# Queries and keys of a head pair: loaded as they lie, with the heads put side by side by GpSimd copies

## The chip, the cores and the metric

One core of a Trainium2 chip. The metric is the device time of one execution of the whole program in microseconds (us), as the median of several runs. The engines are named PE (TensorE), ACT (ScalarE), DVE (VectorE), POOL (GpSimd) and SP (the queue that issues most DMAs).

## What is computed

```python
def _attn_ref(q, k, v):                     # q, k, v: (4, 12, 448, 64) float32
    S = q.shape[2]
    scale = 1.0 / np.sqrt(q.shape[-1])
    scores = scale * np.matmul(q, k.transpose(0, 1, 3, 2)) - np.log(S)
    attn = 1.0 / (1.0 + np.exp(-scores))
    return np.matmul(attn, v).astype(np.float32)

def reference(**kwargs):
    ...
    x = np.ascontiguousarray(attn_out.transpose(0, 2, 1, 3)).reshape(B * S, H * D)   # 1792 x 768
    x = _moe_ref(x=x, **moe_kwargs)          # elu(x @ w_in) @ w_out, weights 768 x 2048 and 2048 x 768
    return _moe2_ref(x=x, **moe2_kwargs)     # (h - tanh(h)) @ w_out with h = x @ w_in
```

The four weight matrices arrive with eight bytes per element and are converted to float32 in the kernel.

## The kernel before

**Stages.** The kernel runs attention first, then the two MLPs, each as a Strassen-like product of blocks in which every float32 operand is split into a head and a rest (three matmuls for one product). While attention runs, the first MLP's weights are already loaded, converted, summed into blocks and stored to scratch memory in HBM. Attention lasts to about 197 us of the span.

**A pair of heads.** The 4 x 12 heads make 24 pairs. For each pair n the work is: transposes of q and k to bring the head dimension to the partitions (`transpose`, L302 to L309; key `t`, with w = 1 for k and 0 for q), a split into head and rest (`head` and `rest`, L311 to L324, on ACT and DVE), scores (`scores`, L332, key `s`), sigmoid (`sig`, L352, ACT at L358), products with v (`pv`, L362 to L373, matmul at L369) and a copy out (`xdone`, L374). One pair's time in the plan is `CYCLE` = 6900 ns. The transposes of pair n are planned two cycles before its scores.

**Loads of q and k.** Pairs are loaded in groups of NL = 2 (m = n // 2). Two buffers of q and k alternate between groups: the tile `first` and the tile `kq1` (L197 to L200). Both hold the two heads of a pair side by side for each row, so that a transpose takes 128 adjacent columns. A row of one head is 64 floats, 256 B, in HBM and in the buffer's place between the two heads. `ld_q` (L230) issues four DMAs for a group and `ld_k` (L213) three; each moves four heads, one row of every head into each partition. `ld_kr` (L222) brings the last 64 keys of each head and `ld_v`, `ld_vr` the values. Groups m > 0 use `ld_q` and `ld_k`; the first group has loads of its own (`ld_first`, L239). All these loads but a few of the first group are issued by SP.

**Order.** `Sched` is a planner: each operation has a queue, a cost, the operations it waits for and a due time (`PHASES`, L85). It simulates the queues and emits each engine's instructions in the planned order. Engines and queues then run their instructions strictly in that order, each waiting for its own semaphores. Attention's operations of one queue are also chained in order of due time (L413), SP's loads among them. A load of a group waits for the transposes of the group that used its buffer before (L287, L288).

**Weights beside attention.** `p_load` (DMA at L592) brings a block of the first MLP's second weights, 768 KB, into XB or XA; `p_narrow` converts it in three steps, the first on ACT (L541), the others on DVE (L544, L548); `p_sum` (L601) forms sums and `p_store` (L606) writes them to `p_forms`. Blocks of the first weights go through tile R1a (load at L530), L541 and so on, to `kept_wi` (L560). `first` is used again after attention: a kept block of weights is loaded into it (L528) and GpSimd writes sums into it (L661).

Of the kernel before, what the change touches and what calls it, by code (L numbers as in the profile page):

```python
# [16 lines left out]
class Sched:  # L17
# [73 lines left out]
    ("ldk",): 4000 - 5 * CYCLE, ("ldv",): 3300 - 2 * CYCLE,  # L91
# [8 lines left out]
def kernel(  # L100
# [67 lines left out]
    with tc.manual_schedule():  # L168
# [7 lines left out]
        def attention():  # L176
# [20 lines left out]
            n = 2 * NL * R * D  # L197
            kq = [first, ld_p.tile([128, 2 * n], F32, name="kq1")]
            kl = [t[:, :n].rearrange("p (c h d) -> p c h d", h=2 * NL, c=R) for t in kq]
            ql = [t[:SP, n:2 * n].rearrange("p (r h d) -> p r h d", h=2 * NL, r=R) for t in kq]  # L200
# [3 lines left out]
            for i in range(2):  # L204
                nc.gpsimd.memset(kl[i][RS:128, R - 1, 0::2, :], 0.0)
                nc.gpsimd.memset(kl[i][0:RS, R - 1, 1::2, :], 0.0)
# [6 lines left out]
            def ld_k(m, i0, i1):  # L213
                b, hp = pairs[NL * m]
                h0, h1 = 2 * hp + 2 * i0, 2 * hp + 2 * i1
                for c in range(3):
                    nc.sync.dma_start(
                        out=kl[m % 2][:, c, 2 * i0:2 * i1, :],
                        in_=k[b, h0:h1, 0:384].rearrange("h (p c) d -> c p h d", c=3)[c],
                    )  # L220

            def ld_kr(m):  # L222
                b, hp = pairs[NL * m]
                for j in range(2):
                    nc.sync.dma_start(
                        out=kl[m % 2][RS * j:RS * j + RS, R - 1, j::2, :],
                        in_=k[b, 2 * hp + j:2 * hp + 2 * NL:2, 384:S].rearrange("h p d -> p h d"),
                    )

            def ld_q(m, i0, i1):  # L230
                b, hp = pairs[NL * m]
                h0, h1 = 2 * hp + 2 * i0, 2 * hp + 2 * i1
                for r in range(R):
                    nc.sync.dma_start(
                        out=ql[m % 2][:, r, 2 * i0:2 * i1, :],
                        in_=q[b, h0:h1].rearrange("h (p r) d -> r p h d", r=R)[r],
                    )

            def ld_first(kind, i):  # L239

                b, hp = pairs[i]
                for j in range(2):
                    if kind == "k":
                        nc.sync.dma_start(
                            out=kl[0][:, :3, 2 * i + j], in_=k[b, 2 * hp + j, 0:384].rearrange("(p c) d -> p c d", c=3)
                        )
                    else:
                        (nc.sync if i else nc.scalar).dma_start(
                            out=ql[0][:, :, 2 * i + j], in_=q[b, 2 * hp + j].rearrange("(p r) d -> p r d", r=R)
# [23 lines left out]
            def loads(m):  # L273


                both = (0, NL)
# [1199 lines left out]
```

## Time and profile before

| | |
|---|---|
| time, median of 3 runs | 1025.57 us (1024.84 to 1026.34) |
| the profiled execution | 1025.25 us |
| its span, first to last instruction | 1023.5 us |
| PE busy | 990.7 us (97%), 5300 matmuls |
| DVE busy | 763.9 us |
| ACT busy | 600.8 us |
| POOL busy | 79.4 us, 74 instructions |
| mean granted TensorE clock | 0.992 |
| DMA packets | 171263, of these 58672 under 512 B |

Busy time counts instructions that an engine executes, not its issuing of DMAs and not its waits. The page says which engine works most over the whole program, and there PE is nearly full. It doesn't say what a single stage is held by: that is read from a stretch of the trace, from the waits of the engines in it and from the chain of work that ended last, which is followed back from the end to whatever released each step. Names such as `kq<-in_q_dram` mean: written tile, from what is read.

### The profile page before, as it was taken

The page shows a single profiled execution, that of the slowest core. Times are in us where ns is not written, and L with a number is a line of the kernel's source. Part 1 is how long each engine was busy: PE and PEld are TensorE (multiplying, and loading weights), DVE is VectorE, ACT ScalarE, POOL GpSimd, SP SyncE. Part 2 cuts the span into 40 slices and gives each one's busy share as a digit, 9 for nine tenths or more (in the row PEclk, how much of TensorE's full clock was granted, in tenths as well). Part 3 has the DMA queues.
Part 4 walks back from the last instruction along what each step waited for, and adds up shares of the span by engine and source line. Part 5 has one row for each costly group of instructions (what it writes and reads, how often), then busy time and mean ns, then how long its engine had stood idle before and what let it go on. Part 6 is the DMA issues. An engine that isn't in the chain of part 4 may idle for free.

```text
span 1023.5 us, 15546 instructions
## 1 busy us (share of the span) xinstructions
PE 990.7 (97%) x5300; PEld 855.4 (84%) x5300; DVE 763.9 (75%) x1155; ACT 600.8 (59%) x966; POOL 79.4 (8%) x74
## 2 busy tenths in 40 slices
PE   8969899989999999999999999999999999999998
PEld 6535455678888888888899998888888999999998
DVE  3657677898888888768878789777777779566673
ACT  4746567876666667666667565444444546445652
POOL 0000000012222220000000021111111000000000
PEclk9989899999999999999999999999999999999999
DMA  7889897025555569999994733555555894455442
GB/s 196 240 253 302 250 285 219 16 80 190 189 188 188 188 203 316 380 412 411 345 328 125 247 109 111 191 190 191 187 194 184 304 335 160 136 174 170 125 143 89
DMA packets 171263, 218.61 MB, mean 214 GB/s; under 512 B 58672, under 2 KB 129584, under 8 KB 170928
## 3 DMA queue, kind: packets, MB, share of 16 engines
q1 hardware_dynamic: 169616, 217.04, 63.8%
q8 instruction: 41, 0.67, 0.3%
q10 hardware_dynamic: 1568, 0.59, 0.2%
q14 instruction: 38, 0.31, 0.1%
HBM read 142.61 MB, written 74.97 MB: 213 GB/s over the span
## 4 chain that ended last, share of the span: by engine, by line
PE 89%; DMA 5%; DVE 3%; ACT 1%; issue 1%; SPq 1%; ACTq 0%; DVEq 0%
PE psa L746 12%; PE psd L746 11%; PE psx L746 9%; PE psu L901 7%; PE psv L901 7%; PE psw L901 7%; PE pvps L369 6%; PE psa L901 6%; PE psb L901 6%; PE psb L746 5%; PE psy L901 4%; PE sps L344 3%; PE psx L901 3%; DMA p_forms<-XB 2%; PE sps L309 2%; DMA R1a<-in_moe_w_in_dram 1%
## 5 line engine op out<-in xcount | busy, mean ns | idle before, releaser
L358 ACT ACTIVATE an<-sps,bias 128x896 f32<-128x896 f32 x72 | 67.3, 1005 | 34.1 <-PE sps L344 33.9
L873 ACT ACTIVATE XB<-t 128x384 fp32r<-128x384 f32 (+1 forms) x111 | 62.0, 563 | 40.8 <-PE psw L901 11.7
L877 DVE TENSOR_TENSOR XB<-t,XB 128x384 fp32r<-128x384 f32 (+1 forms) x111 | 68.3, 625 | 13.2 <-ACT XB L873 13.0
L661 POOL TENSOR_TENSOR second<-second 128x384 f32<-128x384 f32 x15 | 19.0, 1269 | 709.1 <-DVE second L548 213.6
L369 PE MATMUL pvps<-an,vl 128*64 128x448 f32 x288 | 62.7, 573 | 0.0
L873 ACT ACTIVATE XB<-spare 128x512 fp32r<-128x512 f32 (+1 forms) x72 | 41.1, 572 | 26.9 <-PE psw L901 6.6
L344 PEld LDWEIGHTS sps<-e 64*128 64x128 f32 x432 | 39.9, 189 | 18.9 <-PE pvps L369 15.5
L746 PE MATMUL psa<-XB,W 128*128 128x512 f32 x192 | 54.2, 391 | 0.0
L344 PE MATMUL sps<-e 64*128 64x448 f32 x432 | 51.3, 380 | 0.0
L877 DVE TENSOR_TENSOR XB<-spare,XB 128x512 fp32r<-128x512 f32 (+1 forms) x72 | 44.2, 621 | 9.2 <-ACT XB L873 8.8
L901 PE MATMUL psu<-XB,XB 128*128 128x384 f32 (+1 forms) x192 | 46.3, 348 | 0.0
L901 PE MATMUL psv<-XB,XB 128*128 128x384 f32 (+1 forms) x192 | 46.2, 348 | 0.0
L901 PE MATMUL psw<-XB,XB 128*128 128x384 f32 (+1 forms) x192 | 46.2, 348 | 0.0
L369 PEld LDWEIGHTS pvps<-an,vl 128*64 128x64 f32 x288 | 19.5, 144 | 28.5 <-issue 21.1
L746 PEld LDWEIGHTS psa<-XB,W 128*128 128x128 f32 x192 | 36.0, 188 | 7.5
L775 ACT ACTIVATE spare<-t 128x512 f32<-128x512 f32 (+1 forms) x33 | 19.0, 579 | 37.2 <-DVE t L763 36.1
L661 POOL TENSOR_TENSOR first<-first,second 128x384 f32<-128x384 f32 x30 | 40.1, 1335 | 1.2
L317 DVE CAST e<-sps 128x448 fp32r<-128x448 f32 x24 | 15.0, 624 | 30.4 <-PE sps L309 19.3
L746 PE MATMUL psd<-XB,W 128*128 128x512 f32 x144 | 35.7, 391 | 1.5 <-DVE W L678 1.3
L779 ACT ACTIVATE spare<-spare 128x512 f32<-128x512 f32 (+1 forms) x64 | 36.6, 572 | 0.7
L901 PE MATMUL psa<-XB,XB 128*128 128x384 f32 (+1 forms) x156 | 36.9, 347 | 0.0
L901 PE MATMUL psb<-XB,XB 128*128 128x384 f32 (+1 forms) x156 | 36.9, 347 | 0.0
(362 smaller groups left out, 2717.7 us busy)
## 6 DMA issues: line engine op xcount, KB each, us to landing
x_forms<-R1b SPq DMA_DIRECT2D x58, 256.0 KB, 2.0
first<-p_forms SPq DMA_DIRECT2D x36, 384.0 KB, 6.1
t<-x_forms SPq DMA_DIRECT2D x64, 192.0 KB, 2.9
t<-x_forms SPq DMA_DIRECT2D x47, 256.0 KB, 5.0
x_forms<-t SPq DMA_DIRECT2D x44, 256.0 KB, 2.0
x_forms<-R1b SPq DMA_DIRECT2D x58, 192.0 KB, 4.8
first<-in_moe_w_in_dram SPq DMA_DIRECT2D x14, 768.0 KB, 5.3
second<-in_moe_w_in_dram SPq DMA_DIRECT2D x14, 768.0 KB, 6.2
```

The costliest lines, as they stand in the source:

```text
L309: nc.tensor.transpose(ps[:, c * P:(c + 1) * P], t[:, c, h:h + 2, :], ident[:P, :P])
L317: nc.vector.tensor_copy(out=to, in_=x)
L344: nc.tensor.matmul(out=ps[:, j, :S], lhsT=e[lanes, ks, cols], rhs=e[lanes, qs, :S], start=(x == 0), stop=(x == 2),)
L358: nc.scalar.activation(out=a[:, :m], in_=T.pop(("s", n, u))[:, :m, :S], func=ACTF.Sigmoid, bias=bias, scale=scale)
L369: nc.tensor.matmul(out=ps[D * j:D * j + D], lhsT=vl[n // NL % NVL][:, n % NL, 5 * j + u if u < 3 else 3 + j], rhs=a[:, j if u < 3 else 0], ...
L661: by.tensor_tensor(out=out, in0=x, in1=y, op=op)
L746: nc.tensor.matmul(out=ps, lhsT=w[wz][:, k0:k0 + 128], rhs=xs[xz][:, kk], start=(opens and n == 0), stop=(n == 3 * KH - 1), skip_group_che ...
L775: nc.scalar.activation(out=r, in_=h, func=ACTF.Tanh)
L779: nc.scalar.activation(out=r, in_=r, func=ACTF.Exp, scale=-1.0)
L873: nc.scalar.activation(out=at_place(og_place[i, s, p, j], 0, i)[:, :HW[s]], in_=T["graw", i, s, p, j], func=ACTF.Copy)
L877: nc.vector.tensor_tensor(out=lo, in0=T.pop(("graw", i, s, p, j)), in1=f(hi), op=ALU.subtract)
L901: nc.tensor.matmul(out=T["o2", tag], lhsT=lhsT, rhs=rhs, start=(p in OPENS and j == 0 and x == 0), stop=(j == NG - 1 and x == 2), skip_gro ...
```

## The change

Groups m > 0 no longer use `ld_q` and `ld_k`. For each pair and each of q and k, one DMA (`ld_qk`) brings both heads in the rows in which they lie in HBM: four rows of q (1024 B) or three of k (768 B) of a head behind each other in one partition. They go to a new tile `raw_qk` with room for two pairs. A copy on GpSimd (`side_by_side`) then writes them into the layout that the transposes read, with the two heads side by side. The prepared q and k now have one buffer of two pairs, in the tile `first`; the last 64 keys (`krest`) keep two. The load of pair n waits for the copy of pair n - 2, the copy for its load and for the transposes of pair n - 2, and the transposes for the copy. In the plan the load is due at the pair's cycle less four, plus 1000 ns, the copies at less three, plus 4500 and 4600 ns. The first two pairs are loaded as before, straight into `first`.

```diff
--- before.py
+++ after.py
@@ -88,7 +88,7 @@
     ("sig", 0): 700, ("sig", 1): 1700, ("sig", 2): 2700, ("sig", 3): 3700,
     ("head", 1): 4400 - 2 * CYCLE, ("head", 0): 4900 - 2 * CYCLE,
     ("rest", 1): 5050 - 2 * CYCLE, ("rest", 0): 5700 - 2 * CYCLE, ("xdone",): CYCLE + 500,
-    ("ldk",): 4000 - 5 * CYCLE, ("ldv",): 3300 - 2 * CYCLE,
+    ("ldk",): 4000 - 5 * CYCLE, ("ldqk",): 1000 - 4 * CYCLE, ("side", 1): 4500 - 3 * CYCLE, ("side", 0): 4600 - 3 * CYCLE, ("ldv",): 3300 - 2 * CYCLE,
 }
 
 SHIFTS = {
@@ -194,46 +194,45 @@
                 out=ident, in_=ident, pattern=[[-1, 128]], compare_op=ALU.is_equal, fill=0.0,
                 base=0, channel_multiplier=1,
             )
-            n = 2 * NL * R * D
-            kq = [first, ld_p.tile([128, 2 * n], F32, name="kq1")]
-            kl = [t[:, :n].rearrange("p (c h d) -> p c h d", h=2 * NL, c=R) for t in kq]
-            ql = [t[:SP, n:2 * n].rearrange("p (r h d) -> p r h d", h=2 * NL, r=R) for t in kq]
+
+            DD = 2 * D
+            raw_qk = ld_p.tile([128, 4 * NL * R * D], F32, name="raw_qk")
+
+            def parted(t):
+                a, b = NL * R * DD, NL * (R + 3) * DD
+                return t[:SP, :a], t[:, a:b], t[:, b:b + NL * DD].rearrange("p (i x) -> p i x", i=NL)
+
+            (ql, kl, rest0), (qraw, kraw, rest1) = parted(first), parted(raw_qk)
+            krest = rest0, rest1
+            ql, kl = (t.rearrange("p (i c x) -> p i c x", i=NL, x=DD) for t in (ql, kl))
+            qraw, kraw = (t.rearrange("p (i h x) -> p i h x", i=NL, h=2) for t in (qraw, kraw))
             vl = [vs_p.tile([128, NL, 10, D], F32, name=f"vl{i}") for i in range(NVL)]
 
             es = [e0, ld_p.tile([128, 4, 512], F32R, name="e1")]
             for i in range(2):
-                nc.gpsimd.memset(kl[i][RS:128, R - 1, 0::2, :], 0.0)
-                nc.gpsimd.memset(kl[i][0:RS, R - 1, 1::2, :], 0.0)
+                nc.gpsimd.memset(krest[i][RS:128, :, :D], 0.0)
+                nc.gpsimd.memset(krest[i][0:RS, :, D:], 0.0)
             for i in range(NVL):
                 nc.gpsimd.memset(vl[i][RS:128, :, 3, :], 0.0)
                 nc.gpsimd.memset(vl[i][0:RS, :, 4, :], 0.0)
 
             T = {}
 
-            def ld_k(m, i0, i1):
-                b, hp = pairs[NL * m]
-                h0, h1 = 2 * hp + 2 * i0, 2 * hp + 2 * i1
-                for c in range(3):
-                    nc.sync.dma_start(
-                        out=kl[m % 2][:, c, 2 * i0:2 * i1, :],
-                        in_=k[b, h0:h1, 0:384].rearrange("h (p c) d -> c p h d", c=3)[c],
-                    )
+            def ld_qk(w, n):
+                b, hp = pairs[n]
+                x = k[b, 2 * hp:2 * hp + 2, 0:384].rearrange("h (p c) d -> p h (c d)", c=3) if w else q[b, 2 * hp:2 * hp + 2].rearrange("h (p r) d -> p h (r d)", r=R)
+                nc.sync.dma_start(out=(qraw, kraw)[w][:, n % NL], in_=x)
+
+            def side_by_side(n, w):
+                x = (qraw, kraw)[w][:, n % NL].rearrange("p h (c d) -> p c h d", d=D)
+                nc.gpsimd.tensor_copy(out=(ql, kl)[w][:, n % NL].rearrange("p c (h d) -> p c h d", h=2), in_=x)
 
             def ld_kr(m):
                 b, hp = pairs[NL * m]
                 for j in range(2):
                     nc.sync.dma_start(
-                        out=kl[m % 2][RS * j:RS * j + RS, R - 1, j::2, :],
+                        out=krest[m % 2][RS * j:RS * j + RS, :, D * j:D * j + D],
                         in_=k[b, 2 * hp + j:2 * hp + 2 * NL:2, 384:S].rearrange("h p d -> p h d"),
-                    )
-
-            def ld_q(m, i0, i1):
-                b, hp = pairs[NL * m]
-                h0, h1 = 2 * hp + 2 * i0, 2 * hp + 2 * i1
-                for r in range(R):
-                    nc.sync.dma_start(
-                        out=ql[m % 2][:, r, 2 * i0:2 * i1, :],
-                        in_=q[b, h0:h1].rearrange("h (p r) d -> r p h d", r=R)[r],
                     )
 
             def ld_first(kind, i):
@@ -242,11 +241,11 @@
                 for j in range(2):
                     if kind == "k":
                         nc.sync.dma_start(
-                            out=kl[0][:, :3, 2 * i + j], in_=k[b, 2 * hp + j, 0:384].rearrange("(p c) d -> p c d", c=3)
+                            out=kl[:, i, :, D * j:D * j + D], in_=k[b, 2 * hp + j, 0:384].rearrange("(p c) d -> p c d", c=3)
                         )
                     else:
                         (nc.sync if i else nc.scalar).dma_start(
-                            out=ql[0][:, :, 2 * i + j], in_=q[b, 2 * hp + j].rearrange("(p r) d -> p r d", r=R)
+                            out=ql[:, i, :, D * j:D * j + D], in_=q[b, 2 * hp + j].rearrange("(p r) d -> p r d", r=R)
                         )
 
             def ld_v(m, i):
@@ -273,10 +272,9 @@
             def loads(m):
 
 
-                both = (0, NL)
-                kinds = {"kfirst": lambda m, i: ld_first("k", i), "qfirst": lambda m, i: ld_first("q", i), "k": ld_k, "kr": ld_kr, "q": ld_q, "v": ld_v, "vr": ld_vr}
+                kinds = {"kfirst": lambda m, i: ld_first("k", i), "qfirst": lambda m, i: ld_first("q", i), "kr": ld_kr, "v": ld_v, "vr": ld_vr}
                 if m:
-                    jobs = [("q", both), ("k", both), ("kr", ()), ("v", (0,)), ("vr", ()), ("v", (1,))]
+                    jobs = [("kr", ()), ("v", (0,)), ("vr", ()), ("v", (1,))]
                 else:
                     ld_first("q", 0)
                     nc.scalar.activation(out=warm, in_=bias, func=ACTF.Sigmoid)
@@ -287,7 +285,7 @@
                     free = {"k": (2, ("t", 1)), "q": (2, ("t", 0)), "v": (NVL, ("pv", 3))}[kind[0]]
                     last = [(free[1][0], NL * (m - free[0]) + i) + free[1][1:] for i in range(NL)]
                     sch.op(
-                        ("ld" + kind, m) + args, "SP", 600 * {"kfirst": 2, "qfirst": 2, "k": 3, "kr": 2, "q": 4, "v": 1, "vr": 2}[kind],
+                        ("ld" + kind, m) + args, "SP", 600 * {"kfirst": 2, "qfirst": 2, "kr": 2, "v": 1, "vr": 2}[kind],
                         lambda kind=kind, args=args: kinds[kind](m, *args),
                         last, when("ldv" if kind[0] == "v" else "ldk", NL * m) + x, 2500,
                     )
@@ -296,7 +294,7 @@
                 m, i = divmod(n, NL)
                 if kind == "v":
                     return [("ldv", m, i), ("ldvr", m)]
-                part = ("ld" + kind, m, 0, NL) if m else ("ld" + kind + "first", 0, i)
+                part = ("side", n, "qk".index(kind)) if m else ("ld" + kind + "first", 0, i)
                 return [part] + ([("ldkr", m)] if kind == "k" else [])
 
             def transpose(n, w):
@@ -304,9 +302,9 @@
                     T["tps", n] = pss[(4 * n - 5) % 3].tile([128, 2, BK], F32, tag="s", name="sps")
                 T["t", n, w] = ps = T["tps", n][:, w]
                 P, t = ((SP, ql), (128, kl))[w]
-                t, h = t[n // NL % 2], 2 * (n % NL)
                 for c in range(R):
-                    nc.tensor.transpose(ps[:, c * P:(c + 1) * P], t[:, c, h:h + 2, :], ident[:P, :P])
+                    x = krest[n // NL % 2][:, n % NL] if w and c == 3 else t[:, n % NL, c]
+                    nc.tensor.transpose(ps[:, c * P:(c + 1) * P], x, ident[:P, :P])
 
             def head(n, w):
                 W, slot = ((S, 1), (512, 2))[w]
@@ -397,6 +395,9 @@
                     sch.op(("warm", 0), "PE", 100, lambda: keep_warm(WARM), [], -10 ** 9)
                 used = [("s", n - 2, u) for u in range(4)]
                 for w in (1, 0):
+                    if n >= NL:
+                        sch.op(("ldqk", n, w), "SP", 600, lambda n=n, w=w: ld_qk(w, n), [("side", n - NL, w)], when("ldqk", n) - w, 5000)
+                        op("side", n, (w,), "POOL", 1400, side_by_side, [("ldqk", n, w), ("t", n - NL, w)])
                     op("t", n, (w,), "PE", (420, 440)[w], transpose, loaded("qk"[w], n) + before_s(n - 2, 3))
                     op("head", n, (w,), ("DVE", "ACT")[w], (620, 600)[w], head, [("t", n, w)] + used)
                     op("rest", n, (w,), "DVE", (620, 690)[w], rest, [("head", n, w)])
```

## Rows read from the trace of the kernel before

**Rows 1.** Attention, busy us: PE, PEld, DVE, ACT, POOL; clock, DMA share, GB/s.

```profile
12.00:175.00 163.00, 145.36 (x921) 85.69 (x918) 103.72 (x180) 102.85 (x135) 0.00 (x0) 0.96 0.88 258
```

**Rows 2.** Chain that ended last, attention: start us, us, what.

```profile
15.18 3.16 PE pvps L369 x16
...
28.81 3.16 PE pvps L369 x16
...
35.63 3.16 PE pvps L369 x16
...
55.18 13.80 DMA R1a<-in_moe_w_in_dram
...
108.27 11.31 DMA p_forms<-XB
...
188.21 3.16 PE pvps L369 x16
...
194.21 3.18 PE pvps L369 x16
```

**Rows 3.** PE's timeline after the longest waits: start us, us [idle before <-releaser].

```profile
70.84 1.86 PE L309 MATMUL sps<-ident,first 128*128 128x128 f32 x8 [7.81 <-ACT an L358]
...
104.01 1.04 PE L309 MATMUL sps<-ident,first 128*128 128x128 f32 x8 [4.05 <-ACT an L358]
...
122.02 1.83 PE L309 MATMUL sps<-ident,kq 128*128 128x128 f32 x8 [2.46 <-ACT an L358]
...
153.92 1.04 PE L309 MATMUL sps<-ident,kq 128*128 128x128 f32 x8 [2.29 <-ACT an L358]
```

**Rows 4.** ACT's waits, 12 to 200 us: us in total, times, longest.

```profile
ACT R1b L541 <- DMA R1a<-in_moe_w_in_dram: 12.0, 2, 9.2
ACT XB L541 <- DMA p_forms<-XB: 11.8, 4, 5.3
```

**Rows 5.** SP: a wait, its timeline, one line's issues (min/median/max ns).

```profile
SPq L234 <- PE sps L309: 10.4, 9, 3.7
...
56.31 9.98 SPq L234 DMA_DIRECT2D kq<-in_q_dram  x4
...
L217 SPq DMA_DIRECT2D kq<-in_k_dram x18: 484/507/3067, 9.2 to 164.0; - x18
```

**Rows 6.** Queue 1, 10-15, 25-30, 560-580 us (packets, MB, share); q landings.

```profile
q1 hardware_dynamic: 3721, 0.92, 81.3%
...
q1 hardware_dynamic: 1011, 1.93, 102.1%
...
q1 hardware_dynamic: 3070, 4.42, 68.2%
...
kq<-in_q_dram SPq DMA_DIRECT2D x20, 112.0 KB, 8.1
```

**Rows 7.** POOL by form, 0 to 10 us: busy us, mean ns.

```profile
L193 POOL TENSOR_SCALAR_AFFINE_SELECT ident<-ident 128x128 f32<-128x128 f32 x1 | 0.3, 292 | 0.1
...
L1460 POOL MEMSET const-uint8-127<- 128x1 uint8 x1 | 0.1, 112 | 0.0
```

**Rows 8.** Timeline of DVE and POOL after attention, POOL idle, then busy.

```profile
242.84 0.68 DVE L808 TENSOR_TENSOR spare<-spare,t 128x512 f32<-128x512 f32 x1
...
244.52 1.34 POOL L661 TENSOR_TENSOR second<-second 128x384 f32<-128x384 f32 x1 [36.38 <-DVE second L548]
...
245.02 1.38 DVE L808 TENSOR_TENSOR R1b<-t,spare 128x512 f32<-128x512 f32 x1
```

**Rows 9.** Timeline: the first transposes, and tile first after attention.

```profile
9.41 0.95 PE L309 MATMUL sps<-ident,first 112*128 112x112 f32 x4 [0.91 <-DMA first<-in_q_dram]
...
14.20 0.98 PE L309 MATMUL sps<-ident,kq 128*128 128x128 f32 x8
...
173.75 0.46 SPq L528 DMA_DIRECT2D first<-kept_wi  x1
...
204.23 1.33 POOL L661 TENSOR_TENSOR first<-first,second 128x384 f32<-128x384 f32 x1
```

## What bounds the kernel, what the change costs and brings

> **What bounds the kernel now.** I read the stretches first, to see which stage can give anything. From 12 to 175 us, the attention stage, TensorE is busy 145.4 of 163 us while the DMA engines are busy 0.88 of the time [rows 1]. So neither is full, and the loss lies in how they wait for each other. The chain gives the pace: the products with v of two neighbouring pairs start at 28.81 and 35.63, so a pair costs 6.82 us when nothing stops it, and 6.00 us for the last two, which have no transposes beside them [rows 2]. From the first pair's start (15.18) to the last one's (194.21) are 23 steps. At full pace they would take 21 x 6.82 + 2 x 6.00 = 155.2 us; they took 179.0. **The stage therefore loses 23.8 us**, and no faster loading can give more.
>
> TensorE's own timeline shows the form of the loss: four waits of 7.81, 4.05, 2.46 and 2.29 us in front of transposes, all ended by the sigmoid (ACT, L358) [rows 3]. With two short ones they make 17.6 us. The other 6.2 us are slower work after the waits: the eight transposes behind the first and third took 1.86 and 1.83 us, behind the second and fourth 1.04 [rows 3], and the mean granted clock of the stretch is 0.96 [rows 1]. I book 1.85 us of this to each of the three longest waits and 0.6 to the others.
>
> ScalarE is not the cause. Its waits name DMAs: 12.0 us for the weight block R1a and 11.8 us for the stores p_forms, both in front of the conversion at L541 [rows 4]. A sigmoid queued behind L541 waits with it, and TensorE behind the sigmoid. The chain shows those transfers: 13.80 us from issue to landing for the one issued at 55.18, 11.31 for the one at 108.27 [rows 2]. They share one queue, SP's, with the loads of q and k. There the four q loads of one group take 9.98 us of SP from 56.31 on; a k load takes 0.507 us in the median, but up to 3.067 [rows 5]. Part of that is waiting for a buffer: 10.4 us for the transposes alone, the largest of such rows [rows 5].
>
> **What it removes.** For each two pairs after the first two, seven loads (four of q, three of k) with 4 x (448 + 384) = 3328 rows of 256 B go. Four loads with 4 x (112 + 128) = 960 rows of 1024 or 768 B replace them, with the same 0.852 MB. Price of the old: from 10 to 15 us, filled with such rows alone, 3721 packets took 5 us at a share of 0.813 [rows 6]. By the clock that is 4.5 us for a group, by engine time 3.6 us. For rows of 768 and 1024 B no stretch is clean. A mixture of short and long rows moved 4.42 MB in 20 us at 0.682, or 0.324 MB per busy us; one of mostly weights moved 1.93 MB in 5 us at 1.02, or 0.378 [rows 6]. So a group costs 2.6 to 2.25 us. The saving is 1.0 us (3.6 - 2.6) to 2.2 us (4.5 - 2.25) for a group; ten groups fall into this stretch, so 10 to 22 us of DMA time. On SP, four issues at 0.507 take 2.0 us where seven took 3.5 unblocked and the q loads alone up to 9.98 [rows 5].
>
> **What it adds.** 44 copies on GpSimd: 22 of k (128 x 384) and 22 of q (112 x 512). The trace has no such copy. The nearest row with one input is the select of 128 x 128 in 0.292 us [rows 7]; with 0.112 us of fixed part (an estimate: a memset of one column takes that long [rows 7]), that is 1.4 ns for a column, so 0.65 and 0.83 us. The upper end is the two-input operation, 1.34 us for 384 columns [rows 8]: 1.34 and 1.79 us. I take the lower, for the number of inputs. A pair then costs GpSimd 1.5 us (at most 3.1) of its 6.82, and GpSimd has no work of its own in this stage [rows 1].
>
> **What it moves.** A pair's loads are planned at its cycle less four, plus 1.0 us; the copies at less three, plus 4.5; the transposes at less two, plus 3.1. From load to transpose are 15.9 us. A q load lands 8.1 us after issue in this stretch [rows 6]; with both copies 9.6 us, or 11.2 at the upper price, so 4.7 to 6.3 us are spare. What hides it is two pairs of TensorE work, and the cover goes where a load lands later than about 13 us. Second, SP now waits for a copy where it waited for a transpose. Behind it stand v, the weight loads and the stores. The copy of pair n-2 should be over about 2 x 6.82 - 9.6 = 4.0 us before SP needs it, so I count nothing for it, and about 32 us of SP's present buffer waits (four rows, the largest in [rows 5]) largely go. At the start, the first copies follow the first transposes, which end at about 10.4 us (9.41 + 0.95), and are needed at 14.20 [rows 9]; 1.5 to 3.1 us fit.
>
> Third, the tile called first is now read until pair 23's transposes, which come before pair 22's products at 188.21 [rows 2], not until pair 21's; the load of kept weights into it, issued at 173.75, moves behind them. GpSimd first touches that tile at 204.23 [rows 9]. The sixteen us between hide it, so it costs nothing; without that cover it would cost up to 188.2 - 173.8 = 14 us.
>
> **Contention.** While GpSimd worked, a VectorE operation with both inputs in SBUF took 1.38 us where it takes 0.68 without [rows 8]. So a copy may delay such an operation by up to 0.7 us: 44 x 0.7 = 31 us at the very worst. VectorE is idle 163 - 103.7 = 59 us in this stretch [rows 1], and about 36 us if the whole loss vanished. It stays beside the path; I keep 0 to 2 us for it.
>
> The Trainium skill speaks against the copies here (SBUF — State Buffer, "Who interferes with whom"): a VectorE instruction with two SBUF inputs and a GpSimd instruction that reads SBUF exclude each other for a whole instruction. The row of 1.38 us agrees; if every copy held VectorE for its whole length it would be the slower rival below.
>
> **The sum, wait by wait.** Some 80% of the bytes of this stretch (41.9 MB at 258 GB/s over 163 us; q and k are 8.5 of them [rows 1]) are left as they are, so not every wait goes.
> - The wait of 7.81 + 1.85 us hangs on a weight load that itself queues behind other weights; I count half, 4.8.
> - That of 4.05 + 1.85 hangs on a store of 1.3 MB; half, 3.0.
> - That of 2.46 + 1.85 hangs on a store issued right after a group's q and k; all, 4.3.
> - That of 2.29 + 0.2: 1.5. The short ones: 1.4, all.
>
> Together 15.0 us, inside the 10 to 22 us of DMA time. Afterwards the late item is still one of the weight transfers. The stage behind (from 197 us) starts that much earlier and I let it pass the gain on whole, since the last 40 us of attention already run at full pace. The profiled execution took 1025.25 us (span 1023.5 and 1.75 around it), 0.03% from the median of the runs. 1025.25 - 15 = **1010 us**.
>
> **The rivals.**
> - *The whole loss goes* (1001 to 1004): DMA and SP both get slack and 20 to 23.8 us return. For it: 22 us of DMA time at the upper price. Against it: two of the waits hang on bursts of weights. 0.16.
> - *Only the pace of issue changes* (1017 to 1023): the bursts of weights set the waits, and only the short ones and the third vanish, 1.4 + 4.3 less some delay. 0.09.
> - *Nothing*: the rows do not move as long rows, or the queue is refilled at once by weights. 1025, within 2 us. 0.06.
> - *Slower*: VectorE becomes the bound. If each copy holds VectorE's SBUF operations for its whole length at the upper price, 44 x 1.56 = 69 us against 59 us idle; 10 us slower, 1035 us. It decides from 59 / 44 = 1.34 us of delay per copy. For: rows 8 show the exclusion. Against: the seen delay is 0.7, and only part of VectorE's work has two inputs in SBUF. 0.09, with a smaller part of it for a load that lands after 14 us and drags SP round its new loop.
>
> **How the numbers follow.** The forecast (1004 to 1017) has 0.60. The range must leave out no more than 0.2: with the first rival whole and the upper bound set into the second, 1001 to 1019. A measurement of this kernel can tell about 0.2% from no change, 2 us. Faster 0.85, same 0.06, slower 0.09.
>
> **What would show it.** Right: the pairs' starts 6.8 us apart nearly everywhere, last one at about 179 instead of 194; ACT's waits for R1a and p_forms fall from 24 us to under 10; q and k land within 4 us; SP shows no issue over 1 us for them; copies of 0.6 to 0.9 us. Wrong: transposes waiting for GpSimd; SP waiting for POOL; L541 still waiting 9 us for R1a, which would mean the bursts of weights were the cause; or VectorE operations of 1.4 us in numbers and a stage that VectorE fills.

## The result: 1010 us, and attention's last pair 16 us earlier

| | before | after |
|---|---|---|
| time, median (lowest to highest) of 4 runs | 1025.95 us (1024.84 to 1028.15) | 1009.86 us (1008.13 to 1010.57) |
| ratio, 95% interval | | 0.9838 (0.9817 to 0.9859) |
| profiled execution; its span | 1025.25; 1023.5 us | 1008.13; 1006.4 us |
| start of the first and the last pair's products with v | 15.18, 194.21 us | 15.23, 178.19 us |
| POOL busy | 79.4 us | 109.9 us |

The forecast was 1010.0, between 1001 and 1019. The gain lies in the stage where it was looked for. This is attention after the change, in the columns of [rows 1]:

```profile
12.00:175.00 163.00, 156.10 (x1015) 91.89 (x1011) 123.17 (x206) 116.83 (x157) 30.05 (x43) 0.99 0.80 261
```

TensorE does 10.7 us more work in the same 163 us, at a clock of 0.99 where it had 0.96. VectorE and ScalarE do 19 and 14 us more, mostly because more of the stage's work now fits into the window. Next, TensorE's timeline: the two longest waits in front of transposes, with the first and the last pair (start us, us, [idle before <-releaser]).

```profile
15.23 2.10 PE L367 MATMUL pvps<-an,vl 128*64 128x448 f32 x10
...
84.05 1.01 PE L307 MATMUL sps<-ident,first 128*128 128x128 f32 x8 [1.40 <-POOL first L228]
...
109.24 0.87 PE L307 MATMUL sps<-ident,first 128*128 128x128 f32 x3 [4.54 <-ACT an L356]
...
178.19 2.48 PE L367 MATMUL pvps<-an,vl 128*64 128x448 f32 x12
```

Where four waits of 2.3 to 7.8 us stood [rows 3], one of 4.54 us is left, and there is a new one of 1.40 us that a copy on GpSimd ends. From first to last pair are 178.19 - 15.23 = 163.0 us. Without any loss it would be 155.2, so 7.8 of the 23.8 us of loss are left. ScalarE's waits for DMAs tell which part went (12 to 200 us: total, times, longest), to be read against [rows 4]:

```profile
ACT XB L542 <- DMA p_forms<-XB: 9.1, 4, 5.1
ACT R1b L542 <- DMA R1a<-in_moe_w_in_dram: 0.9, 2, 0.6
```

The wait for the weight block R1a went from 12.0 to 0.9 us. The one for the stores went only from 11.8 to 9.1. These are the last two of the four loads of R1a on SP's timeline (start us, us), then the last one of the kernel before, whose third is the one at 55.18 in [rows 2]:

```profile
43.54 0.40 SPq L531 DMA_DIRECT2D R1a<-in_moe_w_in_dram  x1
...
60.57 2.06 SPq L531 DMA_DIRECT2D R1a<-in_moe_w_in_dram  x1
```

```profile
74.67 0.48 SPq L530 DMA_DIRECT2D R1a<-in_moe_w_in_dram  x1
```

The third is issued 11.6 us earlier and the fourth 14.1. The third also takes less time from issue to landing, 7.5 us (it lands at 51.01) where it took 13.80. The copies and VectorE's 32 sums beside them (busy us, mean ns | idle before, its releasers):

```profile
L228 POOL COPY first<-raw_qk 112x512 f32<-112x512 f32 x22 | 17.9, 812 | 11.9 <-DMA raw_qk<-in_q_dram 11.5 <-POOL first L228 0.2
L228 POOL COPY first<-raw_qk 128x384 f32<-128x384 f32 x22 | 13.1, 598 | 107.6 <-DMA raw_qk<-in_k_dram 77.8 <-PE sps L307 28.9 <-PE spq L342 0.9
```

```profile
L602 DVE TENSOR_TENSOR XB<-XB 128x384 f32<-128x384 f32 x32 | 17.5, 569 | 0.1
```

GpSimd spends most of its idle time before a copy waiting for the load, not for a free place. The loads themselves, from 12 to 175 us (count, KB, median us from issue to landing), and the DMA queue between 15 and 20 us, a stretch of nearly only long rows (356 of its 1983 packets are under 512 B), to be read against [rows 6]:

```profile
raw_qk<-in_q_dram SPq DMA_DIRECT2D x20, 224.0 KB, 5.1
...
raw_qk<-in_k_dram SPq DMA_DIRECT2D x20, 192.0 KB, 5.6
```

```profile
q1 hardware_dynamic: 1983, 1.51, 98.8%
```

Five us at a share of 0.988 moved 1.51 MB, or 0.306 MB per busy us. A group's 0.852 MB thus costs 2.8 us, or 2.7 by the packets of 768 and 1024 B alone (2.11 us of the 16 engines' time for 865 and 2.49 for 762; a group has 512 and 448). Last, SP (12 to 175 us: total, times, longest; then one issue of its timeline):

```profile
SPq L224 <- POOL first L228: 6.4, 10, 1.5
...
SPq L264 <- DMA XA<-in_moe_w_out_dram: 4.8, 4, 2.2
SPq L264 <- DMA XB<-in_moe_w_out_dram: 4.4, 3, 1.9
SPq L224 <- DMA p_forms<-XB: 4.3, 2, 2.9
SPq L224 <- DMA R1a<-in_moe_w_in_dram: 3.9, 3, 1.9
```

```profile
37.79 1.59 SPq L224 DMA_DIRECT2D raw_qk<-in_q_dram  x1
```

Rows such as the last four of the first fence are new. A load of q, k or v waits for the end of a weight transfer that it has nothing to do with. In the built program the DMAs of SP and ScalarE take eight semaphores in turn, and a DMA issued by SP waits for the one eight places earlier: the k load at 51.07 us follows by 0.06 us the landing of the R1a load issued at 43.54, the eighth before it. The trace of before shows no such wait between 12 and 160 us, that of after 30.0 us in all. Before, SP stood inside its issues instead. Taken one by one, 156 DMAs held it for 137.1 us, 0.88 us each, and after the change 140 for 86.8 us, 0.62 each. Part of that is waiting for another engine inside the issue, mostly for a buffer, 41.5 and 19.6 us; without it 0.61 and 0.48 us for each are left.

So the time came out as forecast, but not each of its causes. The change does two things at once that the forecast had priced very differently: the rows become longer, and the loads of a group on SP's queue become four instead of seven. The forecast booked nearly all to the rows.

### The profile page after: what moved, and what is told of

It is laid out like the page before. It is cut to its first block, busy times and chain, and to the rows that moved or that the text cites. A ratio compares the mean times of both kernels' runs of the same rounds, so it can differ in the third digit from the quotient of the medians.

```text
span 1006.4 us, 15623 instructions
## 1 busy us (share of the span) xinstructions
PE 985.9 (98%) x5300; PEld 852.9 (85%) x5300; DVE 768.1 (76%) x1155; ACT 600.8 (60%) x966; POOL 109.9 (11%) x118
## 4 chain that ended last, share of the span: by engine, by line
PE 78%; DVE 1%; issue 0%; ACT 0%; DVEq 0%
PE psa L747 12%; PE psd L747 11%; PE psx L747 10%; PE psu L902 7%; PE psv L902 7%; PE psw L902 7%; PE psa L902 6%; PE psb L902 6%; PE psb L747 5%; PE psy L902 5%; PE psx L902 3%; PE psd L902 1%; DVE R1b L809 0%; DVE t L792 0%; DVE R1b L792 0%
## 5 line engine op out<-in xcount | busy, mean ns | idle before, releaser
L874 ACT ACTIVATE XB<-t 128x384 fp32r<-128x384 f32 (+1 forms) x111 | 62.1, 563 | 40.6 <-PE psw L902 10.4
L367 PE MATMUL pvps<-an,vl 128*64 128x448 f32 x288 | 60.1, 552 | 0.0
L228 POOL COPY first<-raw_qk 128x384 f32<-128x384 f32 (+1 forms) x44 | 30.6, 705 | 119.4 <-DMA raw_qk<-in_k_dram 77.8
```

Source lines behind the costliest of these rows:

```text
L228: nc.gpsimd.tensor_copy(out=(ql, kl)[w][:, n % NL].rearrange("p c (h d) -> p c h d", h=2), in_=x)
L367: nc.tensor.matmul(out=ps[D * j:D * j + D], lhsT=vl[n // NL % NVL][:, n % NL, 5 * j + u if u < 3 else 3 + j], rhs=a[:, j if u < 3 else 0], ...
L874: nc.scalar.activation(out=at_place(og_place[i, s, p, j], 0, i)[:, :HW[s]], in_=T["graw", i, s, p, j], func=ACTF.Copy)
```

## The experiments

All were timed in three rounds against the kernel before. Kernels that ran in one group share a chip and are compared by their medians; across groups I compare the ratios to the kernel before. "Loads of a group" counts those of q and k (without the last keys) for two pairs.

| kernel | loads of a group, bytes of a row | median us | ratio (95%) |
|---|---|---|---|
| before | 7, 256 | 1025.95 to 1028.29 | 1 |
| short_split (group 1) | 8, 256 | 1023.87 | 0.9965 (0.9942 to 0.9988) |
| long_split (1) | 8, 768 to 1024 | 1017.98 | 0.989 (0.9861 to 0.992) |
| copies_twice (1) | 4, long | 1007.83 | 0.9791 (0.9753 to 0.9829) |
| no_copies (1) | 4, long | 1009.53 | 0.9809 (0.9777 to 0.9842) |
| after | 4, long | 1009.86 | 0.9838 (0.9817 to 0.9859) |
| long_group (2) | 2, long | 1003.49 | 0.9786 (0.9765 to 0.9807) |
| group_v (2) | 2, long; one of v less | 1003.03 | 0.9779 (0.9753 to 0.9805) |
| pool_issue (2) | 4, long, by GpSimd | 1006.10 | 0.9817 (0.979 to 0.9844) |
| no_loads (2) | 0 from pair 4 on | 1000.53 | 0.9757 (0.9737 to 0.9777) |
| short4 (3) | 4, 256 | 1016.44 | 0.9885 (0.9863 to 0.9906) |
| tiny_loads (3) | 4, long, and 4 needless on SP | 1019.78 | 0.9917 (0.9891 to 0.9942) |
| tiny_pool (3) | 4, long, and 4 needless on GpSimd | 1006.06 | 0.9801 (0.9766 to 0.9836) |
| rests_pool (4) | 4, long; four others moved to GpSimd | 1000.98 | 0.974 (0.9708 to 0.9772) |

### The number of loads against the length of rows: long_split and short_split

Both split each load by head, so that a group has eight loads, one more than before. In the first the rows stay long; in the second every row is a piece of 256 B again, as before the change, and the copies on GpSimd move straight.

```diff
-                nc.sync.dma_start(out=(qraw, kraw)[w][:, n % NL], in_=x)
+                for j in range(2):      # x: head j alone
+                    nc.sync.dma_start(out=(qraw, kraw)[w][:, n % NL, j], in_=x)
...
+                    nc.sync.dma_start(out=(qraw, kraw)[w][:, n % NL, :, D * j:D * j + D], in_=x)   # short_split
```

> The changed kernel, but each long load of a pair is cut by head into two DMAs: rows of 1024 and 768 B as before the cut, eight DMAs for two pairs in place of four (the kernel before had seven). Theory of the rows (the gain comes from the time that the DMA engines spend on 256 B rows): within 2 us of the changed kernel's 1010, so a ratio to the kernel before of 0.983 to 0.987. Rival of the issues (the gain comes from SP issuing four DMAs where it issued seven): the gain is gone, 1020 to 1028.

> As long_split, with the same eight DMAs, tiles, copies, waits and order, but each DMA writes its head's rows at their places between the two heads, so that every piece is 256 B; the GpSimd copies become straight copies of the same size. Theory of the rows: the gain goes back, 1019 to 1028, with pairs again losing some 20 us to waits for weights. Rivals of the issues, of the finer pieces by pair and of the new order: the same time as long_split, within 2 us.

On one chip: 1023.87 with eight short loads, 1017.98 with eight long ones, and 1007.83 with four long ones (copies_twice, below). The rows alone give 5.9 us, the number of loads 10.2. These are the waits in long_split (12 to 200 us):

```profile
PE sps L308 <- ACT an L357: 11.0, 5, 4.0
```

```profile
ACT XB L543 <- DMA p_forms<-XB: 12.9, 4, 4.8
ACT R1b L543 <- DMA R1a<-in_moe_w_in_dram: 5.1, 1, 5.1
```

Long rows with eight loads leave ScalarE's wait for the stores as long as it was before the change, and TensorE behind it. If the rows were the whole cause, this kernel would stand at 1010. If the number were, it would stand at 1026 or later. It stands between: both count. short_split, with one load more than before, is still 3.6 us faster than before (0.0035 x 1026). What else the change does (whole pairs, one buffer and a copy, another due time) is therefore worth something too; it was not tried by itself. One part of it can be read: SP's waits for other engines inside its issues (12 to 160 us) are 12.2 us here and 41.5 before.

### The copies: copies_twice and no_copies

```diff
+                for _ in range(2):      # copies_twice
                     nc.gpsimd.tensor_copy(out=(ql, kl)[w][:, n % NL]..., in_=x)
```

```diff
-                    x = krest[...][:, n % NL] if w and c == 3 else t[:, n % NL, c]     # no_copies
+                    x = krest[...][:, n % NL] if w and c == 3 else t[:, n % NL, c * DD:(c + 1) * DD]
```

> The changed kernel with every GpSimd copy made twice (88 copies, some 61 us of GpSimd in place of 31). Theory that the copies are hidden: 0 to 3 us more than the changed kernel, 1010 to 1013, since a second copy delays VectorE by at most 0.7 us now and then. Rival that the copies cost through VectorE or through later transposes: as much again as they cost now; if that is 5 us, 1015 or more, with transposes that wait for GpSimd in the trace.

> The changed kernel without the copies: the transposes read the long rows where the loads put them, so that a transpose takes two rows of one head in place of one row of two heads (the putting side by side is left out), and the loads of a pair wait for the transposes of the pair four before it, in two buffers. Theory that the copies are hidden: within 2 us of the changed kernel, 1008 to 1012. Rival that they cost by themselves or by the wait of the next load for a copy: 3 us or more faster than the changed kernel, 1001 to 1007.

Twice the copies took 1007.83 us and none 1009.53: their order is even reversed, and the runs of the two overlap (1006.18 to 1010.19 and 1007.62 to 1011.78). First copies_twice, then no_copies, 12 to 175 us, in the columns of [rows 1]:

```profile
12.00:175.00 163.00, 155.89 (x1011) 91.96 (x1013) 126.46 (x206) 116.18 (x155) 60.70 (x87) 0.98 0.80 261
```

```profile
12.00:175.00 163.00, 158.05 (x1015) 92.36 (x1013) 116.91 (x202) 115.39 (x154) 0.00 (x0) 0.98 0.80 261
```

GpSimd's busy time goes from 0 over 30 to 61 us, and VectorE's from 116.9 over 123.2 to 126.5. The windows do not hold quite the same work (202 and 206 instructions of VectorE); over the whole program VectorE's busy time is 764.3, 768.1 and 771.6 us. So the copies do slow VectorE, by some 4 us for each 30 us of them, and it stays beside the path. That the copies are free here is shown to within some 3 us, which is what these runs can tell. What covers them is VectorE's idle time, 36.5 us of these 163 even with twice the copies.

### Fewer loads: long_group, group_v and no_loads

long_group brings both pairs of a group in one load of q and one of k. group_v also joins the two large loads of v. no_loads issues no q and k after the first four pairs, as the way to see the stage without them.

```diff
-                nc.sync.dma_start(out=(qraw, kraw)[w][:, n % NL], in_=x)
+                nc.sync.dma_start(out=(qraw, kraw)[w].rearrange("p i h x -> p (i h) x"), in_=x)   # 4 heads
...
-                        sch.op(("ldqk", n, w), "SP", 600, ..., [("side", n - NL, w)], ...)
+                        if n % NL == 0:
+                            sch.op(("ldqk", n, w), "SP", 600, ..., [("side", n - x, w) for x in (2, 1)], ...)
```

> The changed kernel with one load of q and one of k for two pairs at once (rows of 1024 and 768 B as before, two DMAs for two pairs in place of four; the copies stay by pair). The built program lets a DMA of SP start only when the eighth one before it has landed, so every load of q and k takes one of eight places from the weights. Theory of the places (rows and number of loads both count, since eight long loads gave 1018 and four 1010): another 2 to 6 us less, 1004 to 1008, and SP's waits for earlier DMAs before it issues, some 30 us in the changed kernel from 12 to 160 us, fall to 20 or less. Theory of the rows alone: the same bytes in the same rows, 1010 within 2. Rival that loading two pairs at once makes the transposes late: 1013 or more.

> As long_group, and the values of two pairs in one DMA in place of two (seven loads of q, k and v for two pairs in place of ten in the changed kernel). Theory of the places: 0 to 3 us less than long_group, at best the 1002 at which attention runs at full pace. Theory of the rows alone: as the changed kernel, 1010 within 2.

> The changed kernel without the long loads of q and k from pair 4 on (the copies go on with the rows of pairs 2 and 3, so scores of later pairs are of wrong rows). It prices all that is left of these loads. Theory that DMA bytes and places are the bound of this stage: the loss of about 8 us left in attention goes, 1001 to 1004. Rival that the remaining waits hang on the weights' own order (load, conversion, store): 1006 to 1010.

no_loads gives the floor, 1000.53. long_group reaches 1003.49 with the same bytes and rows as the change; its window and its last pair's products with v, then the window of no_loads:

```profile
12.00:175.00 163.00, 161.86 (x1055) 95.36 (x1056) 122.86 (x210) 122.22 (x163) 25.36 (x44) 1.00 0.79 262
```

```profile
171.06 2.48 PE L368 MATMUL pvps<-an,vl 128*64 128x448 f32 x12
```

```profile
12.00:175.00 163.00, 162.04 (x1058) 95.57 (x1057) 124.20 (x213) 123.94 (x168) 24.03 (x44) 1.00 0.63 212
```

The DMA engines are as busy in long_group as after the change (0.79 against 0.80) and TensorE does not wait all the same. What is left of the loss after the change is therefore no matter of bytes, rows or DMA time. In long_group the last pair starts at 171.06, 155.15 us after the first. It also loads every second pair a cycle earlier, which was not tried by itself. group_v has one load less still and gives no more that can be told (1003.03, with runs from 1001.95 to 1006.74; the slowest was profiled, and its pairs took 159.4 us).

### Who issues: pool_issue, tiny_loads, tiny_pool

pool_issue has GpSimd issue the loads of q and k. The other two add, ahead of each long load, a needless one of 16 x 16 B, issued by SP or by GpSimd.

```diff
-                nc.sync.dma_start(out=(qraw, kraw)[w][:, n % NL], in_=x)
+                nc.gpsimd.dma_start(out=(qraw, kraw)[w][:, n % NL], in_=x)      # pool_issue
...
+                nc.sync.dma_start(out=tiny[:16, 4 * s:4 * s + 4], in_=q[b, 2 * hp, :16, :4])   # tiny_loads; tiny_pool: nc.gpsimd
```

> The changed kernel with the long loads of q and k issued by GpSimd's queue in place of SP's; everything else, the number of loads too, is the same. Theory of the places: SP's eight places are left to weights and v, and it gains as much as long_group or more, 1002 to 1007. Theory of the rows alone: 1010 within 2. Rival that GpSimd's own issuing is slow and holds its copies back: transposes wait for GpSimd, 1012 or more.

> The changed kernel with one needless load of 16 pieces of 16 B in front of each long load of q and k, on the same queue (SP). So SP issues eight DMAs for two pairs, as in long_split, but the long loads stay whole and the bytes grow by nothing that counts. Theory of the places (each DMA of SP takes one of eight places and SP's turn, whatever it moves): as long_split, 1015 to 1021. Theory that the pieces were the cost (two DMAs of half size keep the DMA engines less busy than one): as the changed kernel, 1008 to 1012.

> As tiny_loads, with the needless loads issued by GpSimd, which has places of its own in the built program and a turn of its own. Theory of the places: 1008 to 1013, as the changed kernel. Rival that any further DMA costs on the DMA engines, whoever issues it: as tiny_loads.

The needless loads carry 44 x 256 B in all. On GpSimd's queue they cost nothing that shows (1006.06; ratio 0.9801, beside 0.979 to 0.984 of the other kernels with four long loads). On SP's queue the kernel takes 1019.78, 13.7 us more on the same chip and 8 us more than after by the ratios: 0.2 to 0.3 us for each load. TensorE's waits (12 to 200 us), first tiny_loads, then tiny_pool:

```profile
PE sps L310 <- ACT an L359: 6.6, 4, 2.7
PE sps L310 <- POOL first L231: 5.8, 2, 3.4
```

```profile
PE sps L310 <- ACT an L359: 3.1, 3, 1.6
PE sps L310 <- POOL first L231: 1.4, 1, 1.4
```

And the place where the delay builds up, the last two of the four loads of R1a on SP's timeline, in the same order (start us, us):

```profile
49.29 0.37 SPq L534 DMA_DIRECT2D R1a<-in_moe_w_in_dram  x1
67.97 0.48 SPq L534 DMA_DIRECT2D R1a<-in_moe_w_in_dram  x1
```

```profile
44.05 0.40 SPq L534 DMA_DIRECT2D R1a<-in_moe_w_in_dram  x1
62.72 0.48 SPq L534 DMA_DIRECT2D R1a<-in_moe_w_in_dram  x1
```

With the needless loads on SP these weights are issued 5 us later. The bytes are the same, the order of the other DMAs on SP is the same, and so is the DMA share (0.80 in both).

pool_issue took 1006.10, though it runs at full pace: its last pair starts 155.9 us after its first. But the first one starts at 19.68, 4.4 us late. GpSimd issues the loads of the third and fourth pair at 3.3 to 6.2 us. The loads of the second pair, which SP issues in that time, land later than after the change (k at 10.10 instead of 7.28 us, q at 12.42 instead of 8.94), and TensorE's transposes of the second pair wait for them:

```profile
10.23 1.08 PE L307 MATMUL sps<-ident,first 128*128 128x128 f32 x4 [3.16 <-DMA first<-in_k_dram]
12.55 0.98 PE L307 MATMUL sps<-ident,first 112*128 112x112 f32 x4 [1.24 <-DMA first<-in_q_dram]
```

On SP the loads of the third and fourth pair had stood in line behind these. A queue with nothing else in it can also issue too early.

### Rows at four loads: short4

Whole loads as in the change, four to a group, but in rows of 256 B, with straight copies.

```diff
-                x = k[...].rearrange("h (p c) d -> p h (c d)", c=3) if w else ...
-                nc.sync.dma_start(out=(qraw, kraw)[w][:, n % NL], in_=x)
+                x = k[...].rearrange("h (p c) d -> p c h d", c=3) if w else ...
+                nc.sync.dma_start(out=(qraw, kraw)[w][:, n % NL].rearrange("p c (h d) -> p c h d", h=2), in_=x)
```

> The changed kernel with four loads for two pairs as it has, whole, but each piece written at its place between the heads, so 256 B pieces in place of 768 and 1024 B; copies become straight copies. This is the rows alone, at the changed kernel's number of loads. From short_split against long_split (1023.9 to 1018.0) the rows cost 6 us at eight loads. Theory that rows and places add up: 1014 to 1019. Rival that short rows cost nothing when the loads are few: 1010 within 2. Rival that the rows are nearly all of it: 1022 or more.

1016.44, or 0.9885. Beside after (0.9838) and the others with four long loads (down to 0.979) the rows are worth 5 to 10 us here (10.4 beside tiny_pool on the same chip), at eight loads 5.9. Between short_split and short4, which differ only in the number of loads, lie 0.008, or 8 us. TensorE's wait for ScalarE is again what is left, and ScalarE's for the stores:

```profile
PE sps L308 <- ACT an L357: 9.8, 3, 6.4
```

```profile
ACT XB L543 <- DMA p_forms<-XB: 10.4, 5, 3.9
```

The number of loads and the rows are thus worth about as much, 5 to 10 us each between the kernels compared here. Of the change's own 16.6 us (0.0162 x 1026), the step from before to short4 has 11.8: seven loads to four, and what else the change does. The step from short4 to after, the rows alone, has 4.8. The parts do not simply add, since no kernel gets clearly below the floor.

### Other loads off SP: rests_pool

If any load on SP costs, moving others must help too. Here the loads of q and k stay as in the change. The four small ones of a group, 32 KB each (the last 64 keys and values), are issued by GpSimd from the third group on, so that nothing is early at the start.

```diff
-                    nc.sync.dma_start(
+                    (nc.gpsimd if m > 1 else nc.sync).dma_start(      # ld_kr
...
-                by = nc.sync if m else nc.scalar
+                by = nc.gpsimd if m > 1 else nc.sync if m else nc.scalar      # ld_vr
```

> The changed kernel with the small loads of the last 64 keys and values of each head (four DMAs of 32 KB for two pairs, from group 2 on) issued by GpSimd in place of SP; the loads of q and k stay as they are, and all bytes and rows too. Theory that what counts beside the rows is how many DMAs stand on SP's queue, whatever they load: as long_group and pool_issue, 1002 to 1007. Rival that it was something about the loads of q and k themselves (their size, or their two pairs at once): as the changed kernel, 1008 to 1012. Rival that GpSimd's issuing holds its copies back: slower than that, with transposes that wait for GpSimd.

1000.98 us (1000.41 to 1001.22), ratio 0.974 (0.9708 to 0.9772): the fastest kernel that computes everything, 10 us below the change by the ratios (0.9838 - 0.974), for some 40 loads that moved. Its window (GpSimd's count and busy time hold its 38 DMA issues too), its last pair's products with v, ScalarE's largest wait for a DMA and SP's last load of R1a:

```profile
12.00:175.00 163.00, 161.34 (x1055) 94.73 (x1052) 128.40 (x212) 122.75 (x166) 51.05 (x81) 1.00 0.78 263
```

```profile
171.25 2.48 PE L367 MATMUL pvps<-an,vl 128*64 128x448 f32 x12
```

```profile
ACT XB L542 <- DMA p_forms<-XB: 2.5, 2, 2.0
```

```profile
55.34 1.64 SPq L531 DMA_DIRECT2D R1a<-in_moe_w_in_dram  x1
```

That load is issued at 55.34 where it was 60.57 after the change and 74.67 before. The last pair starts at 171.25, 156.0 us after the first; next to nothing of the loss is left. The Trainium skill (DMA: Bandwidth & Descriptors, "Issuing engines are not separate DMA queues") says that issuing from several engines saves only the sequencer's time to initiate, usually small beside the DMA. The trace agrees on the size of one issue, a median of 0.6 to 0.84 us for these loads after the change, and on the DMA share, which barely moved. But moving some 40 of them gave 10 us of 1010: the issue is short beside one DMA, and yet one load fewer on SP helped what SP issues after it.

### What stays open

Why a load on SP costs 0.2 to 0.3 us of the program. Three things come with each: the time SP spends on issuing it, a place among the eight DMAs that may be under way, since SP holds the next one back until the eighth before it has landed, and its packets' turn in SP's DMA queue, which the traces call q1. GpSimd's loads travel in another one, so moving them changes all three at once. This is that queue in rests_pool (12 to 160 us: packets, MB, share):

```profile
q0 software_dynamic: 1219, 1.25, 2.7%
```

The sum of SP's waits for earlier DMAs (12 to 160 us) does not decide it: 30.0 us after the change, 32.4 in tiny_loads, 30.2 in tiny_pool, 27 in pool_issue, which runs at full pace, but 21.1 in rests_pool and 6.5 in long_group. SP's time inside issues, without the waits in them, does not either: 83.1 us in tiny_loads against 67.2 after the change and 64.1 in long_group, but 99.7 in short4, which is no slower than tiny_loads. The two together do follow the times: 50 to 76 us in the kernels that come near the floor (no_loads, group_v, long_group, rests_pool, pool_issue), 94 to 97 in those with four long loads on SP, 100 in short4, 115 and 116 in tiny_loads and long_split, 123 in short_split. Only the kernel before stands apart, with 95.6 and the 41.5 us of waits for other engines. So SP's own time as a whole is the likely cause; this is an order over runs and not an experiment. A kernel that lengthens SP's turn without a DMA was not tried.

## Why the prediction was right, and which of its terms were not

- **The bound.** Right. The loss of 23.8 us was all that could be won: no_loads and rests_pool, without loss, stand at 1000.5 and 1001.0, where the rival "the whole loss goes" was put (1001 to 1004).
- **The price of rows.** The term that was mis-sized. Long rows cost 2.7 to 2.8 us for a group, where 2.25 to 2.6 was taken from mixtures, so the saving is 0.8 to 1.8 us of DMA time for a group, or 8 to 18 for ten, not 10 to 22. Only 5 to 10 us came out in the time (short4 and short_split).
- **The loads on SP.** The step that failed. Four issues for seven were written down as 2.0 us for 3.5 and were not carried into the sum as a cause of their own. The number of loads carries as much as the rows: 8 us from eight to four at short rows, 10.2 at long ones. SP runs in order, and the weight loads and stores stand behind the small loads. The rival "only the pace of issue changes" (1017 to 1023) came nearest to this, but let only the short waits and the third go. short4, with fewer loads and no longer rows, stands at 0.9885, or some 1014 us against the median before, so the issue side gave more than that rival allowed. It was no rival but the other half of the cause.
- **Wait by wait.** The total was right, 15.0 forecast and 16.0 us measured, by errors that cancelled: luck in part. The wait for R1a was booked at half and went wholly (12.0 to 0.9 us). It did not hang on a burst of weights alone, but also on when SP got to it: the third load, on which the wait of 7.81 us hung, is issued 11.6 us earlier and lands after 7.5 us instead of 13.80. Which of the two counts for more is not separated. The wait for the store was booked at half, and one of 4.54 us stands where 4.05 stood (a store issued at 95.60 that lands at 106.70). That store moves 1152 KB, not the 1.3 MB written there, and the one behind the third wait was issued at 108.27, ahead of a group's q loads and not right after its q and k. "The late item is still one of the weight transfers" held for the store.
- **The copies.** Right in price (0.60 and 0.81 us against 0.65 and 0.83) and in cost: none, by copies_twice and no_copies.
- **The distance from load to transpose.** The spare time was smaller than worked out. The loads landed after 5.1 and 5.6 us, better than the 8.1 counted on but not within 4, and six of their 40 issues took 1.0 to 1.85 us where none over 1 was foreseen. In five of the six the issue held a wait for a copy (in the row of 37.79 above the copy ended at 39.23, 0.15 us before the issue did). One k load was issued only at 76.55, behind a row of other DMAs, landed 6.2 us later, and its copy at 83.26 made the transposes at 84.05 wait 1.40 us. The cover failed by a late issue, not by a late landing.
- **SP waiting for copies.** Counted at nothing; it was 6.4 us in ten waits of at most 1.5, where 32.3 us of buffer waits had stood in four rows. no_copies has none of them and is no faster.
- **The tile used twice.** Right in its cost: SP's load of kept weights now waits 8.3 us for the last transposes, and nothing behind it shows it. The span fell by 17.1 us, 1.1 more than the last pair moved, so the stage behind passed the whole gain on.
- **Contention and the slower rival.** The rival fell. The rival's mechanism shows, and is small (the mean sum takes 569 ns instead of 549; two took 848 and 858, both beside a copy), VectorE's busy time over the whole program grew by 4.2 us, and its idle time covered it. The rule cited from the Trainium skill (SBUF — State Buffer, "Who interferes with whom") is not contradicted; its price here was about 4 us of VectorE's time beside the path, and 8 with twice the copies.

## What to carry to other kernels

Count the DMAs on a queue as well as their bytes and rows: on a queue that works in order a small load delays the large ones behind it, here even one that moves 256 B. Before reshaping a transfer, try to join loads or to give the small ones to an engine that issues no others; here that was worth as much as the long rows, and long rows with either of the two took the stage to its floor. And check what such an idle queue does at the start: with nothing ahead of its loads, it sends them while the loads that are needed first are still under way.

## What was not expected of the hardware

- A needless load of 256 B cost 0.2 to 0.3 us of the program on SP's queue and nothing that could be measured on GpSimd's (44 of them: 1019.78 against 1006.06).
- Short rows hold the issuing engine. Without the waits inside them, SP's issues took 0.61 us each before, 0.69 in short_split and 0.72 in short4, against 0.48 after the change. With long rows SP gets through its issues and then waits for earlier DMAs instead, 30.0 us where there was none.
- At a DMA share of 0.79 the stage ran without loss (long_group), and at 0.80 it lost 7.8 us: DMA time was not what held it.
